# Two layers of linear attention and MLP on one core: queries projected in quarters, some rows kept on chip, new orders for every engine

## The chip, the cores and the metric

The kernel runs on one core of a Trainium2 chip. The metric is the device time in microseconds (us). Of the kernel before there are three timed runs, 989.24, 989.56 and 990.01 us, with a median of 989.56 us. Besides these there is one execution under the hardware profiler, which took 986.68 us; its trace spans 985.0 us from the first instruction to the last.

## What is computed

The input x has 2048 rows of 512 values. Two layers with the same weights are run, each an attention block and an MLP, both with a layer norm ahead and a residual:

```python
x = x + _A_ref(_layernorm(x), A_wqkv, A_w_phi, A_wo)
x = x + _B_ref(_layernorm(x), B_w1, B_w2)
x = x + _A_ref(_layernorm(x), A_wqkv, A_w_phi, A_wo)
x = x + _B_ref(_layernorm(x), B_w1, B_w2)
```

```python
phi_q = jnp.concatenate([_softmax(pq, axis=-1), _softmax(-pq, axis=-1)], axis=-1)
phi_k = jnp.concatenate([_softmax(pk, axis=-1), _softmax(-pk, axis=-1)], axis=-1)
kv = jnp.einsum("bhsf,bhsd->bhfd", phi_k, v)
z  = jnp.einsum("bhsf->bhf", phi_k)
num = jnp.einsum("bhqf,bhfd->bhqd", phi_q, kv)
den = jnp.einsum("bhqf,bhf->bhq", phi_q, z)[..., None] + 1e-6
o = num / den
```

There are 32 heads of 16. `pq` and `pk` are the queries and keys times a 16x16 matrix per head. kv and z are sums over all 2048 rows, so no row's output of the attention can be worked out before all keys and values have been. The MLP is `relu(x @ w1) @ w2` with 1792 hidden columns.

## The kernel before, in words

**Products.** Every matrix product is done in fp16 with each operand split into a high and a low half, and three matmuls per block (high x high, high x low, low x high; `PAIRS`). A weight W is split by `split`: ScalarE (ACT) writes the high half, scaled by a power of two, and VectorE (DVE) writes the rest (lines 417 and 419). The per-head matrix `w_phi` is folded into the key and the query weight at the start (`fold`, tiles `st_k`, `wt_k`, `pf_k`, `wk_h`, `wk_l` and the same with q). The scales come from the sums of squares of the weights (`square`, `squares_of`, line 370), added up over the partitions by a small matmul (`sb_k`, `sb_v`, line 380).

**Stages.** The 2048 rows are 16 chunks of 128; two chunks are a tile. Layer 0 begins with the *front*: for each chunk the layer norm, the transposed rows `xT` (`front_norm`), keys `pk`, values `pv`, and their part of kv (`gather`). Queries of the first chunks are projected in the front too (`query`, PSUM tile `pq`, line 624, twelve matmuls of 128x512). ACT copies `pq` to `qs` (line 785), SP's queue stores it to `q_dram` (788), and later `look` loads it as `ql` (869), the feature map on DVE, ACT and GpSimd (POOL) makes `e_q`, `fm_q` and `p_q` (653 to 688), and a DMA transpose makes `pT` (553). Rows whose query is projected late are stored to `xt_dram` (718) and loaded again as `xq` (777).

Then stands `opening(l)`, once per layer: the numerators `pn` of the first two chunks (890), the quotient `o`, its transpose `tr_o` (568) and `oT`, the product with wo (`pw`), the layer norm `xn_b`, its transpose `tr_b` and `yT`, and the remaining queries. In layer 0 the opening also holds `warming`: matmuls of the ones against themselves, whose result nobody reads (`warm_kv`, line 1558); `warm_y` are the same ahead of the first weights. After it come eight tiles of MLP steps: hidden products `ph` (1237, 1317), relu halves `h` (ACT 1000, DVE 1003), output products `py` (1351, 1394), and at their sides the attention of later tiles and, in layer 0, the keys and values of layer 1. Some steps use seven products instead of eight blocks; for these the sums of weight blocks `sums` are made on POOL (1110) and the sums of rows `ts`, `n_t`, `n_u` on POOL and ACT (961, 539, 542). `opening(1)` stands between the last tile of layer 0 and the first of layer 1. The last rows end with `mlp_out` (1369) and their store.

**What sets the order.** Every operation is a task of a `Plan` with its engine, its buffers and an estimated time. The tables in `ORDER` give each engine's sequence of tasks outright, as offsets into the list of tasks not yet taken; so each engine runs its own list strictly in that sequence, and an instruction that waits holds up all that stand behind it on its engine. SP issues all DMAs, the transposes among them, in one such list. Buffers rotate: the fp16 rows of the back half (`n16b`) have one place, so that ACT may write `n_t` only when the DMA transpose of the `n_b` before it has read that place.

Of the kernel before, what the change touches and what calls it, by code (L numbers as in the profile page):

```python
# [56 lines left out]
        "00000503111412100011109903770662a5203355172601416019402091430070220630063170300H0260D172320x600105016o00"  # L57
        "1310i1h00f001100000000001013100100004000124034010203406070020045010707992a1a020c370713504413320100001110"
        "00000020002000000000000000050700d00bh000j00k000000000000000000000001111122222222222122222222222022233330"
        "222222201000000001112201004400800b0000000000000011122223220111111111122220111111101112011110000000000003"  # L60
        "0500bbh0000000000000000600000000011122011122222222222333333333334445555555555144440333334445555555577777"
        "788888999aa09aaaaab0aaaa0999999aaaaaaaaaaa09999908006660550033333302222222222822222222222233320112222223"
        "33334444444444455555555555555104402229220pv11y1111111111111111100000000000000000000080035333331201g11000"
        "0aa00802004031010002002200570004000000020000201111122244444444444444444445556666666004550450444403333330"
        "22011111111100005006000000000000000000709000e00000000000000000b0E00000000z000000000000000000000000u00000"
        "000p00000000p00000000000000000000000000d00000000000000000000n0000000000000d0v000000000000000j00000000000"
        "00e0000000000000000000000000020v00w000000000000000000000000000o000000000000f0000000000000000000030000000"
        "000000030000000000000000h00000000000000050000k000k000000000000000000000000000011000000000030000000000000"
        "00000000000000000000000000000000000000000000000000000000000000000000000000000000000000000000000000000000"
        "00000000000000000000000000000000000000000000000000000000",  # L70
    DVE:
        "31203011i1103e4331212321g1001h4b03303304c0014070d01b000d0cWW00e0Sdg44e466e050Gbe5040390x20g1jf111f00g00i"
# [201 lines left out]
def tile_kernel(ctx: ExitStack, tc: tile.TileContext, x_in, wqkv, w_phi, wo, w1, w2, out):  # L274
# [165 lines left out]
    class Slots:  # L440
# [37 lines left out]
        def split(self, i):  # L478
            last = self.last
            split(lambda: self.raw(i, last), S_[f"s_{self.name}"], lambda: self.part(i, 0),  # L480
                  lambda: self.part(i, 1), self.n, [self.at_raw(i)], self.res[i], "")
# [1378 lines left out]
```

## Time and profile before

| | |
|---|---|
| median of the timed runs | 989.56 us (989.24 to 990.01) |
| profiled execution | 986.68 us, span 985.0 us |
| busy, share of the span | PE 98%, DVE 70%, POOL 61%, ACT 55% |
| instructions | PE 9514 matmuls, DVE 1396, ACT 1065, POOL 583 |
| moved by DMA | 182.21 MB, mean 185 GB/s |
| granted TensorE clock | 0.997 of full |

"Busy" is the time in which an engine had an instruction in work. A matmul of 128x512 is listed at 379 ns, but such matmuls start 216 ns apart, so PE busy means that it always had one under way. In the rows of the timeline the first number is the start and the second the duration, both in us; a bracket at the end gives how long the engine was idle just before and what ended that idle time. "x12" is the number of instructions in a row.

### The profile page before, as it was taken

What the parts mean: (1) busy time and instruction counts of PE and PEld (TensorE: products, weight loads), DVE (VectorE), ACT (ScalarE), POOL (GpSimd) and SP (SyncE); (2) the same over time, 40 slices, a digit from 0 to 9 for tenths busy, and PEclk for the clock granted to TensorE, in tenths of its full rate; (3) what the DMA queues carried; (4) which work ended last, traced back from release to release, by engine and by line L of the source; (5) the groups of instructions that cost most, each with busy time, mean ns of one, the idle gap of its engine ahead of it and who ended that gap; (6) DMA issues with size and microseconds to landing.
All of it is one profiled execution on the core that took longest, in us unless ns stands there. A gap on an engine that the chain in (4) does not pass through costs nothing.

```text
span 985.0 us, 23814 instructions
## 1 busy us (share of the span) xinstructions
PE 960.6 (98%) x9514; PEld 655.2 (67%) x9514; DVE 692.6 (70%) x1396; ACT 544.6 (55%) x1065; POOL 601.7 (61%) x583
## 2 busy tenths in 40 slices
PE   8999999999999999999999999979999999999997
PEld 5554555656565666666756565546666798898996
DVE  6889898986867768766564577846887665664554
ACT  7899975453454644544444344544455565564553
POOL 2586973667774856746345344455668788776553
PEclk9999999999999999999999999999999999999999
DMA  8357657659779797887758354899999977765541
GB/s 327 130 164 194 183 161 235 144 149 202 176 188 228 211 198 206 198 194 184 197 108 197 120 161 118 267 187 232 240 245 209 238 172 175 203 161 136 151 147 64
DMA packets 254575, 182.21 MB, mean 185 GB/s; under 512 B 184448, under 2 KB 191872, under 8 KB 254464
## 3 DMA queue, kind: packets, MB, share of 16 engines
q1 hardware_dynamic: 254464, 180.69, 71.2%
q8 instruction: 74, 1.21, 0.5%
q14 instruction: 37, 0.30, 0.1%
HBM read 103.84 MB, written 32.51 MB: 138 GB/s over the span
## 4 chain that ended last, share of the span: by engine, by line
PE 79%; DVE 7%; DMA 4%; ACT 3%; POOL 3%; issue 2%; SPq 1%; DVEq 0%; POOLq 0%; ACTq 0%
PE ph L1237 22%; PE py L1351 16%; PE py L1394 9%; PE pk L624 7%; PE pv L624 7%; PE pw L624 6%; PE pq L624 5%; PE ph L1317 2%; PE pn L890 2%; PE kv L762 2%; DMA oT<-n_o 1%; DVE fm_q L668 1%; DVE e_q L660 1%; SPq L553 1%; POOL p_q L688 1%
## 5 line engine op out<-in xcount | busy, mean ns | idle before, releaser
L1351 PE MATMUL py<-w,h 128*128 128x512 f16 x852 | 215.8, 379 | 0.0
L1237 PEld LDWEIGHTS <-s 128*128 128x128 f16 x2352 | 151.7, 98 | 34.9 <-issue 5.2
L1250 ACT ACTIVATE sn<-ph 128x128 f32<-128x128 f32 x294 | 80.3, 273 | 159.9 <-PE ph L1237 158.6
L624 PEld LDWEIGHTS <-xT 128*128 128x128 f16 x840 | 81.3, 98 | 92.9 <-issue 0.2
L1237 PEld LDWEIGHTS <-w 128*128 128x128 f16 x1764 | 110.7, 98 | 18.9 <-DMA yT<-n_b 2.2
L1351 PEld LDWEIGHTS <-h 128*128 128x128 f16 x852 | 75.5, 98 | 58.4
L1237 PE MATMUL ph<-yT,s 128*128 128x128 f16 x1176 | 97.6, 219 | 3.6 <-DVE ph L1256 2.2
L1237 PE MATMUL ph<-yT,w 128*128 128x128 f16 x1176 | 97.6, 219 | 3.0 <-ACT qs L785 3.0
L677 POOL TENSOR_TENSOR e_q<-e_q,fm_q 128x1024 f32<-128x1024 f32 x32 | 63.7, 1991 | 55.2 <-ACT fm_q L673 53.7
L1256 DVE TENSOR_TENSOR ph<-ph,sn 128x128 f32<-128x128 f32 x98 | 29.2, 298 | 85.5 <-PE ph L1237 42.0
L677 POOL TENSOR_TENSOR e_k<-e_k,fm_k 128x1024 f32<-128x1024 f32 x30 | 58.7, 1957 | 47.2 <-ACT fm_k L673 42.0
L688 POOL TENSOR_TENSOR p_q<-e_q,p_q 128x1024 f16<-128x1024 f32 x32 | 68.7, 2147 | 25.1 <-ACT p_q L684 24.1
L624 PE MATMUL pw<-wo_h,oT 128*128 128x512 f16 x256 | 81.2, 379 | 1.4 <-DMA oT<-n_o 1.4
L624 PE MATMUL pk<-wk_h,xT 128*128 128x512 f16 x256 | 81.3, 379 | 0.0
L624 PE MATMUL pv<-wv_h,xT 128*128 128x512 f16 x256 | 81.0, 379 | 0.0
L688 POOL TENSOR_TENSOR p_k<-e_k,p_k 128x1024 f16<-128x1024 f32 x30 | 65.3, 2177 | 21.4 <-ACT p_k L684 21.3
L1261 DVE TENSOR_TENSOR ph<-ph,sn 128x256 f32<-128x256 f32 x98 | 42.0, 429 | 49.5 <-PE ph L1237 49.2
L624 PE MATMUL pq<-wq_h,xq 128*128 128x512 f16 x208 | 66.8, 384 | 1.8 <-DMA xq<-xt_dram 1.8
L624 PEld LDWEIGHTS <-oT 128*128 128x128 f16 x384 | 36.7, 98 | 42.2 <-DMA oT<-n_o 1.7
L1003 DVE SCALAR_TENSOR_TENSOR h<-ph,h 128x512 f16<-128x512 f32 x71 | 48.0, 678 | 21.5 <-ACT h L1000 20.9
L1050 POOL TENSOR_TENSOR w<-r 128x256 f32<-128x256 f32 x41 | 31.4, 766 | 44.4 <-ACT r L1046 35.2
L1000 ACT ACTIVATE h<-ph 128x512 f16<-128x512 f32 x71 | 41.7, 591 | 26.5 <-DVE ph L1261 22.4
(241 smaller groups left out, 2294.7 us busy)
## 6 DMA issues: line engine op xcount, KB each, us to landing
s<-s_dram SPq DMA_DIRECT2D x98, 512.0 KB, 4.4
q_dram<-qs SPq DMA_DIRECT2D x32, 256.0 KB, 3.4
ql<-q_dram SPq DMA_DIRECT2D x32, 256.0 KB, 3.7
xt_dram<-xT SPq DMA_DIRECT2D x26, 256.0 KB, 4.4
xq<-xt_dram SPq DMA_DIRECT2D x26, 256.0 KB, 3.8
xe<-in_A_x_dram SPq DMA_DIRECT2D x16, 256.0 KB, 5.3
x<-in_A_x_dram SPq DMA_DIRECT2D x16, 256.0 KB, 3.5
x_dram<-x SPq DMA_DIRECT2D x16, 256.0 KB, 4.4
```

What stands on the lines that cost most here:

```text
L624: nc.tensor.matmul(pm.ap, xT.ap[:, a, k, :], W.ap[b][:, k, :], start=(k == 0 and i == 0), stop=(k == KC - 1 and i == 2))
L677: (nc.vector if fast else nc.gpsimd).tensor_tensor(e3, e3, sm.unsqueeze(2).to_broadcast([P, 2 * n, DH]), op=ALU.mult)
L688: (nc.vector if fast else nc.gpsimd).tensor_sub(p16.ap[:, 1, cols], ef, p16.ap[:, 0, cols])
L1000: nc.scalar.activation(h[0].ap, at(), AF.Relu)
L1003: add(DVE, 0.607, lambda: nc.vector.scalar_tensor_tensor(h[1].ap, at(), 0.0, h[0].ap, op0=ALU.max, op1=ALU.subtract), reads=[ph, h[0]], wr ...
L1050: nc.gpsimd.tensor_sub(rf.ap[:, :2, :], r.ap.rearrange("p (a b) -> p a b", a=4)[:, ::3, :], block(1).unsqueeze(1).to_broadcast([P, 2, P]))
L1237: nc.tensor.matmul(at(r), weight_of(i, b, kk, s, summed), rows_of(y, i, a, kk), start=(first and kk == 0 and n == 0), stop=(kk == 1 and n ...
L1250: nc.scalar.activation(saved(i), at(2), AF.Copy)
L1256: add(DVE, 0.27, lambda: nc.vector.tensor_tensor(at(3), at(1), saved(2), op=ALU.add), reads=[(ph, 1), (sn, 2)], writes=[(ph, 3)], boost=10 ...
L1261: add(DVE, 0.40, lambda: nc.vector.tensor_tensor(wide(ph), wide(ph), wide(sn), op=ALU.add), reads=[(sn, 0), (sn, 1)], writes=[(ph, 0), (ph ...
L1351: nc.tensor.matmul(py.ap, h[a].ap.rearrange("p j t -> p (j t)")[:, cols], W2.at(b, fs[j], slice(0, D)), start=(begins and j == k == 0), st ...
L1394: nc.tensor.matmul(py.ap[:, 256 * r:256 * r + 256], left[a], right[b], start=(s == 0 and r == 0 and k == 0), stop=(last and k == 2), skip_ ...
```

## The change

1. **Queries in four pieces.** `project` takes `cuts`; a query's twelve matmuls are four tasks of three, so that the order may put other work between them. The queries of the first six chunks of layer 0 stay whole.
2. **First queries of layer one stay in SBUF.** For chunks 0 to 3 of layer 1 (`straight`) ACT copies `pq` into the `ql` tile itself: four stores to `q_dram` and four loads from it are gone.
3. **Rows not copied through memory.** `direct` now holds for chunks 12 to 15 of layer 0 and 14 and 15 of layer 1 too: six stores to `xt_dram` and six loads from it are gone. Each of these transfers is 256 KB.
4. **Key weight asked for first**: both halves of `st_k` are issued ahead of `phi` and the second chunk's rows. The first chunk's rows still go first in SP's list.
5. **Squares** of a weight are taken in one or two ACT instructions in place of four.
6. **W2's first four pairs** are split on ACT and POOL: two more ACT instructions each, and `tensor_sub` on POOL (new line 425) in place of DVE's line 419.
7. **Warming**: all 29 matmuls in `opening(0)` go, and 6 of 26 at the start.
8. **The last product by halves** (`last_rows`): the last six matmuls of 128x512 become twelve of 128x256 into two PSUM banks, with one DVE instruction and one store for each half.
9. All five `ORDER` tables are new. `opening(1)` now lists the queries of chunks 2, 3, 14 and 15 ahead of the layer norm.

```diff
     def direct(l, c):
-        return l == 0 and c < NCH - LATE
+        return soon(c) or c >= NCH - 2 * CPT if l == 0 else c >= NCH - CPT
+    def straight(l, c):
+        return l == 1 and c < 2 * CPT
...
-    def project(xT, W, tag, name):
+    def project(xT, W, tag, name, cuts=1):
...
-            for k in range(KC):
+            for k in range(part * KC // cuts, (part + 1) * KC // cuts):
...
-        add(PE, 2.59, go, reads=[xT, W], makes=[pm])
+        for part in range(cuts):
+            add(PE, 2.59 / cuts, partial(go, part), reads=[xT, W], makes=[] if part else [pm],
+                writes=[pm] if part else [])
...
-        pq = project(xT, Wq, tag, f"pq_{n}")
-        qs = tiles(fr, "qs", [P, D], F32, f"qs_{n}")
+        pq = project(xT, Wq, tag, f"pq_{n}", cuts=1 if l == 0 and soon(c) else 4)
+        kind = "ql" if straight(l, c) else "qs"
+        qs = tiles(fr, kind, [P, D], F32, f"{kind}_{n}")
...
+        if pool:
+            add(ACT, 0.16 + cols / 1160, lambda: nc.scalar.activation(w(), w(), AF.Copy, scale=s.ap),
+                reads=[s], writes=reads)
+            add(ACT, 0.16 + cols / 1160, lambda: nc.scalar.activation(hi(), w(), AF.Copy),
+                reads=reads, writes=[(res, f"h{key}")])
+            add(POOL, 0.14 + cols / 523, lambda: nc.gpsimd.tensor_sub(lo(), w(), hi()),
+                reads=[*reads, (res, f"h{key}")], writes=[(res, f"l{key}")])
+            return
...
-            square(lambda k=k: f32_piece(b)[:, k, :], lambda k=k: W.ap[1][:, k, :], sq, k, 512,
+            square(lambda ks=ks: f32_piece(b)[:, ks, :], lambda ks=ks: W.ap[1][:, ks, :], sq, i, 512 * n,
...
-        if idle:
-            warming("kv0", 10, before())
+        if l == 1:
+            for c in [*range(CPT, 2 * CPT), *range(NCH - CPT, NCH)]:
+                query(l, c, "h")
```

The order shows what that moves. On **PE in the opening of layer 0** the last numerators of chunk 1 (`pn_1`) are followed by the turns `tr_o` of the two chunks and the product with wo (`pw_0`). Before, from the turn of chunk 1 on:

```order
L568 MATMUL tr_o_1_2170<-ident,o_1_2150 128x128 x4
L1558 LDWEIGHTS ones
L1558 MATMUL warm_kv_6_2122<-ones 128x256
...
L624 LDWEIGHTS oT_0_2163
L624 MATMUL pw_0_2185<-wo_h,oT_0_2163 128x512
```

and after, from the last numerators on:

```order
L916 MATMUL pn_1_0_2093<-rhs_0_2004,pT_1_1891 128x68
L634 LDWEIGHTS xT_12_1396
L634 MATMUL pq_12_2029<-wq_h,xT_12_1396 128x512
...
L577 MATMUL tr_o_0_2118<-ident,o_0_2067 128x128 x4
L634 LDWEIGHTS xT_12_1396
L634 MATMUL pq_12_2029<-wq_h,xT_12_1396 128x512
...
L577 MATMUL tr_o_1_2135<-ident,o_1_2114 128x128 x4
L634 LDWEIGHTS oT_0_2130
L634 MATMUL pw_0_2142<-wo_h,oT_0_2130 128x512
```

Pieces of three matmuls of the query of chunk 12, read from its own `xT`, now stand where groups of warming stood; another piece of that query stands between the numerators, and one of chunk 11 behind `pw`. Before, the queries of chunks 11 and 12 ran whole ahead of the numerators.

On **ACT in the opening of layer 1**, at the layer norm of chunks 0 and 1 (`xn_b`, `n_b`) and the sum of their rows (`n_t`). Before:

```order
L539 ACTIVATE n_b_0_8961<-xn_b_0_8943 128x512
L785 ACTIVATE qs_9_8984<-pq_9_8947 128x512
L602 ACTIVATE xn_b_1_8989<-x_1_8010,stat_b_1_8963 128x512
L539 ACTIVATE n_t_0_9039<-ts_0_8998 128x512
L785 ACTIVATE qs_10_9041<-pq_10_8971 128x512
L539 ACTIVATE n_b_1_9043<-xn_b_1_8989 128x512
L664 ACTIVATE e_q_4_8930<-e_q_4_8930,inv_q 128x1024
L785 ACTIVATE qs_11_9070<-pq_11_9014 128x512
```

and after:

```order
L548 ACTIVATE n_b_0_8876<-xn_b_0_8871 128x512
L806 ACTIVATE qs_6_8884<-pq_6_8797 128x512
L611 ACTIVATE xn_b_1_8895<-x_1_7760,stat_b_1_8867 128x512
L548 ACTIVATE n_b_1_8945<-xn_b_1_8895 128x512
L806 ACTIVATE qs_7_8953<-pq_7_8862 128x512
L548 ACTIVATE n_t_0_8965<-ts_0_8925 128x512
L676 ACTIVATE e_q_4_8892<-e_q_4_8892,inv_q 128x1024
L806 ACTIVATE qs_8_8975<-pq_8_8936 128x512
```

The norm of chunk 1 and one more copy of a query have moved ahead of `n_t`, and the queries around it are 6 to 8 where they were 9 to 11.

On **POOL around the opening of layer 0**, from the feature map of chunk 1's query (`p_q_1`) on. Before:

```order
L688 TENSOR_TENSOR p_q_1_1553<-e_q_1_1026,p_q_1_1553 128x1024
L677 TENSOR_TENSOR e_q_2_1899<-e_q_2_1899,fm_q_2_1898 128x1024
L688 TENSOR_TENSOR p_q_2_2198<-e_q_2_1899,p_q_2_2198 128x1024
L605 TENSOR_TENSOR stat_b_0_2219<-stat_b_0_2219,nhalf 128x1
L677 TENSOR_TENSOR e_q_3_2012<-e_q_3_2012,fm_q_3_2011 128x1024
L605 TENSOR_TENSOR stat_b_1_2242<-stat_b_1_2242,nhalf 128x1
L688 TENSOR_TENSOR p_q_3_2267<-e_q_3_2012,p_q_3_2267 128x1024
```

and after:

```order
L700 TENSOR_TENSOR p_q_1_1763<-e_q_1_1073,p_q_1_1763 128x1024
L425 TENSOR_TENSOR w_0_140<-w_1_141,w_0_140 128x1024
L689 TENSOR_TENSOR e_q_2_1862<-e_q_2_1862,fm_q_2_1861 128x1024
L700 TENSOR_TENSOR p_q_2_2132<-e_q_2_1862,p_q_2_2132 128x1024
L689 TENSOR_TENSOR e_q_3_2011<-e_q_3_2011,fm_q_3_2010 128x1024
L614 TENSOR_TENSOR stat_b_0_2179<-stat_b_0_2179,nhalf 128x1
L1136 TENSOR_TENSOR sums_2035<-sums_2035 128x256
L1136 TENSOR_TENSOR sums_1983<-sums_1983 128x256
L614 TENSOR_TENSOR stat_b_1_2198<-stat_b_1_2198,nhalf 128x1
L700 TENSOR_TENSOR p_q_3_2184<-e_q_3_2011,p_q_3_2184 128x1024
L425 TENSOR_TENSOR w_1_141<-w_2_142,w_1_141 128x1024
```

Two of the four W2 subtractions stand here (`w_0`, `w_1`), the other two some seven instructions apart behind them, and the norm's `stat_b_0` now follows `e_q_3`.

More of the change, by code (lines that the diff above doesn't have):

```diff
@@ L62 @@
[L62 to L66, printed above, removed]
```

196 lines of the change are left out of this document (104 added, 92 removed).

## Prediction

> **What bounds the kernel now.** First the page's busy times, then a table of windows cut at the stages, to see where the busiest engine is not busy.
>
> ```profile
> PE 960.6 (98%) x9514; PEld 655.2 (67%) x9514; DVE 692.6 (70%) x1396; ACT 544.6 (55%) x1065; POOL 601.7 (61%) x583
> core 0: us, PE busy (x) PEld busy (x) DVE busy (x) ACT busy (x) POOL busy (x), PEclk, DMA share, GB/s
> 0.00:22.00 22.00, 17.11 (x109) 12.62 (x110) 13.00 (x41) 15.60 (x36) 5.18 (x17) 1.00 0.88 316
> 22.00:157.00 135.00, 135.00 (x984) 71.40 (x985) 122.54 (x222) 117.05 (x178) 93.24 (x64) 1.00 0.59 172
> 157.00:174.00 17.00, 15.79 (x175) 11.30 (x174) 13.38 (x34) 8.35 (x13) 9.88 (x7) 1.00 0.83 261
> 174.00:205.00 31.00, 30.23 (x248) 19.36 (x246) 29.05 (x48) 16.32 (x23) 20.88 (x18) 1.00 0.65 145
> 205.00:640.00 435.00, 431.42 (x4034) 272.45 (x4034) 302.33 (x596) 205.72 (x396) 241.60 (x209) 1.00 0.73 184
> 640.00:672.00 32.00, 26.06 (x231) 15.27 (x230) 16.64 (x38) 14.43 (x29) 17.88 (x17) 0.95 0.96 201
> 672.00:970.00 298.00, 295.55 (x3662) 245.68 (x3661) 187.75 (x409) 164.28 (x386) 208.50 (x248) 1.00 0.76 187
> 970.00:985.00 15.00, 9.43 (x85) 7.08 (x83) 7.93 (x14) 2.88 (x6) 4.53 (x6) 0.92 0.14 54
> ```
>
> PE is the bound. Its idle time is the window less its busy time: 4.89 us at the start, none in layer 0's front, 1.21 and 0.77 in and behind the first opening, 3.58 in the long middle, 5.94 in the second opening, 2.45 behind that and 5.57 in the last 15 us. That is 24.4 us in all, so no reordering can win much over 20 us, and a change wins only where PE idles, crawls, or does work that nobody reads. The matmuls that compute the result stay the same but for the very last six, which become twelve of half the width. So I go through the four places.
>
> **Start.** The rows are PE's, then two of ACT's on the squares of the value weight, and one group of squares of W2.
>
> ```profile
> 8.26 1.09 PE L1505 MATMUL wt_k<-ident,st_k 128*128 128x128 f32 x8 [0.23 <-DMA st_k<-in_A_wqkv_dram]
> 15.06 0.36 PE L380 MATMUL sb_v<-sq_v,ones 128*128 128x4 f32 x2 [1.09 <-DVE stat_a L607]
> 21.89 1.15 PE L1505 MATMUL wt_q<-ident,st_q 128*128 128x128 f32 x8 [1.38 <-ACT wT_q L1510]
> 14.02 0.63 ACT L370 ACTIVATE wv_l<-st_v 128x512 bf16<-128x512 f32 x1
> 14.54 0.20 ACT L370 ACTIVATION_READ_ACCUMULATOR wv_l<-st_v 128x1 f32 x1
> L370 ACT ACTIVATE w<-w x9: 1041/1049/1692, 39.4 to 98.6; 128x1024 bf16<-128x1024 f32 x6, 128x1792 bf16<-128x1792 f32 x3
> ```
>
> PE is held twice behind ACT's list: `sb_v` needs the last square, finished at 14.74, and `wt_q` waits 1.38 us. A square of 512 columns takes 0.62 us from start to start with its read; two of 1024 save a little (1.05 + 0.19 against 1.24), and one of 2048, by the step from 1024 to 1792 columns (0.64 us for 768) about 1.90 + 0.20, saves about 0.4 of 2.5. More is won because `sb_v` now stands behind all of `pf_k` on PE, so that the splits of the key weight no longer wait for a value square between them. The second half of the key weight, now one place earlier in SP's list, can win no more than PE waits for it, with what follows. The bounds are 0 (ACT's table load now waits for the first rows, and eats the gain) and the 0.23 + 1.09 + 1.38 us that the three brackets hold, 2.7. I take the two larger brackets at about two thirds of their 2.5 us: **-1.7**.
>
> **First opening.** The group row is that of the warming; a piece of the chain of waits gives a query's twelve matmuls; POOL's row shows how loaded it was.
>
> ```profile
> L1558 PE MATMUL warm_kv<-ones x29: 272/273/273, 158.3 to 170.1; 128*128 128x256 f16 x29
> 620.25 2.59 PE pq L624 x12
> 157.20 1.29 PE L890 MATMUL pn<-rhs,pT 128*128 128x68 f16 x36
> 170.88 1.39 PE L1317 MATMUL ph<-yT,w 128*128 128x128 f16 x22 [0.42 <-DVE yT L577]
> 159.74 1.93 POOL L677 TENSOR_TENSOR e_q<-e_q,fm_q 128x1024 f32<-128x1024 f32 x1 [12.08 <-ACT fm_q L673]
> ```
>
> From the numerators at 157.20 to the first hidden product at 170.88 PE follows a chain through DVE, ACT and back, 13.7 us long; warming only filled it. Four pieces of three query matmuls, 12 x 2.59/12 = 2.6 us, move from ahead of that chain into it. If the chain keeps its length, everything after comes 2.6 us earlier. It could also shrink: the warming's stream is 29 x 0.108 = 3.1 us (half a 512-column matmul each). It could stretch: `stat_b_0` now stands behind `e_q_3` on POOL, up to 1.9 us by POOL's row, of which a part falls into idle time. Bounds -3.1 and -0.7 (2.6 less 1.9); I take **-2.6**, since DVE ahead of it has three splits fewer and so does not hold the numerators.
>
> **W2's pairs** stand in and behind this opening.
>
> ```profile
> L419 DVE SCALAR_TENSOR_TENSOR w<-w,s_w,w x9: 1272/1539/2123, 80.8 to 187.5; 128x1024 f16<-128x1024 f32 x6, 128x1792 f16<-128x1792 f32 x3
> L688 POOL TENSOR_TENSOR p_q<-e_q,p_q 128x1024 f16<-128x1024 f32 x32 | 68.7, 2147 | 25.1 <-ACT p_q L684 24.1
> 195.01 2.30 POOL L688 TENSOR_TENSOR p_q<-e_q,p_q 128x1024 f16<-128x1024 f32 x1 [0.66 <-ACT p_q L684]
> 195.25 2.62 DVE L659 TENSOR_TENSOR e_q<-ql,fm_q 128x512 f32<-128x512 f32 x1
> 185.37 0.68 DVE L659 TENSOR_TENSOR e_q<-ql,fm_q 128x512 f32<-128x512 f32 x1
> 205.76 2.78 PE L1317 MATMUL ph<-yT,w 128*128 128x256 f16 x24 [1.53 <-DVE h L1003]
> ```
>
> DVE loses 4 x 1.27 = 5.1 us, three of the four ahead of the numerators and one behind. POOL gains 4 x 2.15 = 8.6 us, at the price of `p_q`, the same shape; ACT gains 8 instructions of 1.05 (the 1024-column row above), 8.4 us. Between 157 and 205 POOL is busy for 30.8 of 48 us and ACT for 24.7; with three of the four pairs POOL has 37.2 and ACT 31.0, so there is room, and the first pair falls into POOL's 12.08 us of idle time. But the two `e_q` rows show what POOL's work does to DVE: beside a POOL instruction of that size 0.68 us became 2.62. Three such meetings would cost DVE 3 x 1.94 = 5.8 us, net of the one saved split +4.5, and PE waits for DVE at 205.76. If none meet, the 1.53 there may go. Bounds: -1.5 and +4.5; most POOL instructions of these 48 us meet no two-input DVE work, so I take **+0.5**, nearer the lower end. If the cover on POOL is gone, PE waits for W2's low halves themselves; that is a rival below.
>
> The Trainium skill has a rule that speaks against this edit: by "SBUF — State Buffer", section "Who interferes with whom", VectorE with two inputs in SBUF and GpSimd exclude each other, and the later one is blocked until the first ends. The two rows agree with it: DVE's instruction ends at 197.87, 0.56 behind POOL's end at 197.31, about the time that it takes by itself. If that rule struck at every pair, the sum would take the upper bound above.
>
> **Second opening.** PE's two stalls and the query after them, ACT's and SP's rows in that place, and the transposes of `yT` between 635 and 660.
>
> ```profile
> 649.77 0.49 PE L1237 MATMUL ph<-yT,w 128*128 128x128 f16 x6 [2.98 <-ACT qs L785]
> 652.13 0.61 PE L624 MATMUL pq<-wq_h,xq 128*128 128x512 f16 x1 [1.49 <-DMA xq<-xt_dram]
> 652.13 4.11 PE pq L624 x12
> 648.60 0.63 ACT L539 ACTIVATE n_t<-ts 128x512 f16<-128x512 f32 x1 [6.48 <-DMA yT<-n_b]
> 642.46 5.82 SPq L553 DMA_TRANSPOSE pT<-p_q  x1
> DMA to landing us min/median/max: 4.1/6.0/8.0
> ```
>
> The bracket at 649.77 names a copy of a query, but ACT's list shows the cause: ACT stood 6.48 us at `n_t`, until the transpose of `n_b` had landed, and the copy that frees PE's bank was queued behind. That transpose took up to 8.0 us while the DMA engines were 0.96 busy; SP sat 5.82 us on the next one, so `xq` was issued late, and PE waited 1.49 us more. Then twelve matmuls took 4.11 us where 2.59 is usual.
>
> After the change, the order puts the norm of chunk 1 and one more copy ahead of `n_t`, and on PE 39 query matmuls and two groups of numerators between `pw` and the first `ph`, where 36 and one stood: 3 x 0.216 + 0.38 = 1.0 us more cover. The `xq` that was late is no longer behind that transpose, and the clock's loss goes with the idle time: 1.0 + 1.49 + (4.11 - 2.59) = 4.0 us. Twelve of the removed 256 KB transfers belong to layer 1's queries; if the transpose lands in the 4.1 us of the faster one, the remaining 2 us go as well. Bounds 0 (the wait only moves to the next transpose) and -7.5 (the stage's 5.94 us and the slow matmuls' 1.5). I take **-4.5**, near the worked 4.0.
>
> **Tail.** DVE's and POOL's last rows.
>
> ```profile
> 978.00 0.47 DVE L1426 SCALAR_TENSOR_TENSOR v<-py,inv,w 128x256 f32<-128x256 f32 x1
> 978.56 2.50 POOL L1434 TENSOR_TENSOR x<-x,v 128x512 f32<-128x512 f32 x2 [6.37 <-DVE v L1426]
> 980.59 1.53 DVE L1369 SCALAR_TENSOR_TENSOR x<-py,inv,x 128x512 f32<-128x512 f32 x3
> ```
>
> The last sums wait for POOL's two additions, which end at 981.06, not for PE; so halving the last product wins nothing. DVE now does one more 0.5 us instruction ahead of what POOL needs: bounds 0 and +1.3 (one whole POOL addition), taken **+0.5**.
>
> **Sum.** -1.7 - 2.6 + 0.5 - 4.5 + 0.5 = -7.8 us. From the profiled execution's 986.68 (span 985.0 and 1.68 around it) this gives 978.9; the median of the timed runs is 2.88 above that execution, so 989.56 - 7.8 = **981.8 us**.
>
> **Rivals.** (A) *The chains set both openings.* If DVE and the transposes, not the place of PE's work, decide when `ph` begins, the queries' pieces fill holes that were waits anyway. For it: ACT's 6.48 us ended with a DMA. Against: PE's order has 1 us more cover, and twelve transfers are gone. It keeps the -0.7 of the first opening, -1.5 of the second and half the start: -3, giving 986.5.
>
> (B) *POOL becomes the bound behind the first opening: slower.* The price is its 8.6 us of subtractions straight on the path, and DVE's net 4.5 from being held, in place of the 0.5 taken: 13.1 - 8.3 = +4.8, giving 994.4 at the worst, and 991.1 if three quarters of it show (9.8 - 8.3 = +1.5), the size that I give the rival; it is slower than before from 8.3 us on. It decides from the point where W2's low half of a step comes after PE is through that step's product with the high half; the stall at 205.76 says that there is no slack in that stage already. Against it stands POOL's 17 us of room in 48.
>
> (C) *All waits go*: start -2.7, first opening -3.1, W2 -1.5, second -7.5, tail 0: -14.8, giving 974.8.
>
> (D) *The clock falls in the first opening.* In the second, 2.98 and 1.49 us of idle time with 0.9 of work between made twelve matmuls 1.52 us slower. Without warming, PE has holes in the first opening: 0.33 us twice and 0.42 before, and up to about 1.5 us where 18 warming matmuls filled the wait around `tr_b`. If these suffice, one such loss comes back: 983.3. The Trainium skill, "TensorE: Matmul & The Clock Gate", section "Part 1: The HAM clock gate (the "warmup" mystery)", states that the clock is halved after an idle window of about 3.4 us; the slow query above agrees with it, and by that rule the holes here are too short.
>
> (E) *It doesn't do what it says*: the first rows still go ahead of the key weight, so the start keeps its time. Then 983.5, inside the forecast's own range.
>
> **Chances.** Forecast with D and E, 979 to 985: 0.58. A, 985 to 989: 0.17. C, below 979: 0.13. B and other slips above 989: 0.12. The range leaves out about 0.2: **975.5 to 989.0**. A measurement of this kernel can tell about 0.2% (2 us) from no change, that is outside 987.6 to 991.5. Faster by that: 0.58 + 0.13 + 0.11 of A = 0.82; within: 0.06 of A and 0.03 of B = 0.09; slower: 0.09.
>
> **What would show it.** Start: `pk` begins at about 15.5 instead of 17.3. First opening: numerators about 4.3 us earlier, and the same 13.7 us from there to the first `ph`. W2: no bracket in front of PE's `py` that names POOL. Second opening: no `pq` at half rate, PE idle under 2 us there, ACT's wait at `n_t` below 4. Tail: POOL's last addition ends later after PE's end than 1.2 us. The forecast is wrong if ACT still waits 6 us at `n_t`, or if DVE's two-input instructions in the first tile grow past 2 us each.

## The result and the profile after

The changed kernel takes **979.83 us** (median of 4 runs, 979.15 to 981.66), against 989.78 us (989.24 to 991.13, 4 runs) for the kernel before beside it. The ratio is 0.990, 95% interval 0.9882 to 0.9918: 1% faster, by 10 us, where -7.8 us and 981.8 us were forecast. Timed again later, beside the last experiment, it gained 6.8 us (981.21 against 987.96 us, ratio 0.9935, interval 0.9916 to 0.9954), so the gain is known to 7 to 10 us. Its profiled execution took 979.16 us with a span of 977.4, 7.6 us less than before.

The table of windows of the kernel after, cut where its own stages begin and end:

```profile
core 0: us, PE busy (x) PEld busy (x) DVE busy (x) ACT busy (x) POOL busy (x), PEclk, DMA share, GB/s
0.00:22.00 22.00, 16.37 (x98) 12.48 (x98) 12.85 (x40) 14.01 (x23) 4.65 (x17) 0.92 0.79 272
22.00:155.50 133.50, 133.04 (x975) 70.65 (x976) 117.28 (x217) 118.00 (x176) 96.08 (x66) 1.00 0.62 176
155.50:173.50 18.00, 15.30 (x157) 9.61 (x156) 16.18 (x34) 10.50 (x15) 11.77 (x9) 1.00 0.65 186
173.50:204.00 30.50, 28.76 (x245) 18.69 (x243) 24.12 (x44) 22.88 (x29) 24.08 (x18) 1.00 0.63 134
204.00:633.00 429.00, 427.81 (x4021) 271.07 (x4019) 298.35 (x590) 203.63 (x392) 238.81 (x208) 1.00 0.68 178
633.00:665.00 32.00, 28.20 (x263) 17.02 (x262) 19.58 (x44) 16.46 (x33) 18.47 (x17) 1.00 0.89 200
665.00:963.00 298.00, 297.12 (x3662) 245.99 (x3660) 190.71 (x412) 164.90 (x388) 212.86 (x250) 1.00 0.78 189
963.00:977.40 14.40, 8.55 (x80) 6.84 (x78) 8.04 (x14) 2.58 (x5) 5.91 (x7) 0.89 0.19 73
```

PE's idle time is now 5.6 us at the start (4.9 before), 2.7 and 1.7 around the first opening (there before's busy time held 3 us of warming), 1.2 in the middle (3.6 before), 3.8 in the second opening (5.9), 0.9 behind it (2.5). The start got worse, and the middle, which the forecast left alone, got better.

To put the terms beside this, both traces are compared at points of **equal useful work**: each matmul row counts its columns (0.216 us for 512 at full clock, 0.111 for an fp32 transpose of 128), warming counts nothing, and the point is when so much had been started. The table gives how the lead of before changes over each stretch, minus being a gain; the last column holds the other profiles of the experiments below whose code in that stretch is the changed kernel's, with their number. Another way of counting the small matmuls shifts an entry by up to 0.1 us.

| stretch, by useful work | forecast | the two profiles | other profiles, same code there |
|---|---|---|---|
| start, 0 to 40 us | -1.7 | +0.94 | +0.80 to +3.81 (8) |
| front, 40 to 140 | 0 | +0.14 | +0.13 to +0.14 |
| first opening, 140 to 156 | -2.6 | -1.68 | -1.68 to -1.69 (4, without e1) |
| W2 and first tile, 156 to 201 | +0.5 | +0.23 | +0.22 to +0.24 (4, without e1) |
| middle, 201 to 590 | 0 | -2.25 | -0.36 to -2.23 (9) |
| second opening, 590 to 643 | -4.5 | -3.94 | -4.11 to -5.59 (9) |
| behind it, 643 to 920 | 0 | -1.33 | -0.33 to -1.65 (10) |
| tail, 920 to the end | +0.5 | +0.29 | +0.25 to +0.39 (10) |
| sum | -7.8 | -7.6 | |

So the total came out near the forecast partly by luck, with errors that offset each other: start, front, openings and W2 came out 4.0 us worse together than forecast, and 3.6 us were gained in stretches that were priced at nothing. In e1 the first opening and the first tile are apart in the table because PE ran at half rate there, from about 171 to 174 us; over both stretches e1 comes out as the first profile does, for it did not meet the wait of 1.74 us shown below. The rows behind the table, stage by stage.

**Start**, in the kernel after: PE's first wait, ACT's first instructions, SP's issue of `phi`.

```profile
8.09 0.50 PE L381 MATMUL sb_phi<-sq_phi,ones 128*128 128x1 f32 x2 [2.19 <-ACT squares L371]
18.03 0.38 PE L634 MATMUL pk<-wk_h,xT 128*128 128x512 f16 x1
```

```profile
3.81 1.28 ACT L611 ACT_TABLE_LOAD   x1 [3.81 <-DMA xe<-in_A_x_dram]
5.77 0.81 ACT L611 ACTIVATE xn_a<-xe,stat_a 128x512 f32<-128x512 f32 x1 [0.68 <-DVE stat_a L616]
7.68 0.26 ACT L371 ACTIVATE squares<-phi 128x64 bf16<-128x64 f32 x1 [1.10 <-DMA phi<-in_A_w_phi_dram]
7.94 1.04 ACT L371 ACTIVATE wk_l<-st_k 128x1024 bf16<-128x1024 f32 x1
```

ACT's table load, which needs no data, stands in the list behind the wait for the first rows, at 3.81; `phi`, now behind 1 MB of key weight, lands about 7.6; the key weight's first square begins at 7.94, where before it began at 5.21. `pk` begins at 18.03, not at the 15.5 forecast. But ACT's list is not all of it:

```profile
10.18 1.75 PE L1551 MATMUL wt_k<-ident,st_k 128*128 128x128 f32 x8
11.28 1.27 ACT L1556 COPY wT_k<-wt_k 128x512 f32<-128x512 f32 x2 [1.17 <-PE wt_k L1551]
```

The same eight transposes took 1.09 us before (the row at 8.26 in the prediction). Behind its wait of 2.19 us PE ran at half rate (PEclk is 0.50 from 9 to 11 us), and ACT, done with its squares, waited 1.17 us for them. All nine profiles with this start show it (1.69 to 1.92 us), the two with before's start (before and e8) do not (1.09). Where `tr_a` behind it still ran near full rate (0.60 to 0.69 us: the first profile, e6, e10) the start is +0.8 to +1.1; where that was slow too (1.02 to 1.06 us: e3, e4, e5, e7, e9, e12) it is +1.5 to +3.8. Before's own start lies 0.97 us apart in its two profiles.

**First opening**, DVE's and POOL's rows at the numerators, then PE's:

```profile
155.10 2.42 DVE L671 TENSOR_TENSOR e_q<-ql,fm_q 128x512 f32<-128x512 f32 x1
172.32 2.62 DVE L672 TENSOR_TENSOR e_q<-fm_q,ql 128x512 f32<-128x512 f32 x1
```

```profile
154.86 2.11 POOL L689 TENSOR_TENSOR e_q<-e_q,fm_q 128x1024 f32<-128x1024 f32 x1 [1.03 <-ACT fm_q L685]
171.80 2.58 POOL L425 TENSOR_TENSOR w<-w,w 128x1024 f16<-128x1024 f32 x1
```

```profile
155.73 0.92 PE L916 MATMUL pn<-rhs,pT 128*128 128x68 f16 x24
159.10 0.41 PE L577 MATMUL tr_o<-ident,o 128*128 128x128 f32 x2 [0.40 <-DVE dn L924]
170.06 1.63 PE L1343 MATMUL ph<-yT,w 128*128 128x128 f16 x24 [1.17 <-ACT qs L806]
175.59 0.54 PE L916 MATMUL pn<-rhs,pT 128*128 128x68 f16 x12 [1.74 <-DVE yT L586]
```

The numerators came earlier by 1.47 us although the start was later, but the quotients waited: DVE's next subtraction, 0.68 us by itself, lasted 2.42 until POOL's product beside it had ended. From the numerators to the end of the first 24 `ph` it is 15.8 us (155.73 to 171.52) where before it was 14.9 (157.20 to 172.11). Behind it the same happens again: POOL's new W2 subtraction of 171.80 holds DVE's `e_q` of 172.32 for 2.62 us, and PE waits 1.74 us at 175.59. The 1.53 us at 205.76 of before are gone, so this stretch comes out even.

**Second opening**: PE's two waits, ACT's `n_t`, SP's transpose ahead of it.

```profile
644.64 0.49 PE L1263 MATMUL ph<-yT,w 128*128 128x128 f16 x6 [1.83 <-ACT qs L806]
648.81 0.51 PE L1263 MATMUL ph<-wk_h,s 128*128 128x128 f16 x6 [1.09 <-DMA wk_h<-n_t]
```

```profile
642.43 0.63 ACT L548 ACTIVATE n_t<-ts 128x512 f16<-128x512 f32 x1 [2.16 <-DMA yT<-n_b]
```

```profile
637.54 1.23 SPq L562 DMA_TRANSPOSE yT<-n_b  x1
```

ACT waits 2.16 us at `n_t` (6.48 before), the transpose lands 4.9 us after its issue (8.0 before), PE waits 1.83 and 1.09 (2.98 and 1.49 before), and no `pq` runs at half rate: PEclk is 1.00 in this window.

**Tail**: DVE's last additions still wait for POOL.

```profile
973.61 0.88 DVE L1414 SCALAR_TENSOR_TENSOR x<-py_last,inv,x 128x256 f32<-128x256 f32 x2 [1.10 <-POOL x L1478]
```

### The profile page after: what moved, and what is told of

The parts are those of the page before. It is cut to its first block, busy times and chain, and to the rows that moved or that the text cites. A ratio compares the mean times of both kernels' runs of the same rounds, so it can differ in the third digit from the quotient of the medians.

```text
span 977.4 us, 23693 instructions
## 1 busy us (share of the span) xinstructions
PE 955.1 (98%) x9485; PEld 652.3 (67%) x9485; DVE 687.1 (70%) x1390; ACT 553.0 (57%) x1057; POOL 612.6 (63%) x587
## 5 line engine op out<-in xcount | busy, mean ns | idle before, releaser
L634 PEld LDWEIGHTS <-xT 128*128 128x128 f16 x912 | 87.5, 98 | 97.9 <-issue 0.4
L634 PE MATMUL pq<-wq_h,xq 128*128 128x512 f16 x160 | 54.1, 379 | 0.0
```

The costliest lines, as they stand in the source:

```text
L634: nc.tensor.matmul(pm.ap, xT.ap[:, a, k, :], W.ap[b][:, k, :], start=(k == 0 and i == 0), stop=(k == KC - 1 and i == 2))
```

## The experiments

All but the last two were run once. The totals of such runs differ by up to 3 us through the start alone (most of that goes with the clock), so each is read in the stretch that it touches. In the diffs `MOVES` takes the task with the first number out of an engine's sequence and puts it ahead of the task with the second.

**e1_phi_between.** `phi` goes between the halves of the key weight.

```diff
-        writes=[phi], kb=32).deps.setdefault(key_load, False)
+        writes=[phi], kb=32)
+MOVES = {SP: [(3, 1)]}
```

> The changed kernel with one place of SP's list as before: phi is issued between the two halves of the key weight, not behind both. In the changed kernel phi lands at about 7.7 us, PE stands 2.19 us at sb_phi, and the first value product begins at 22.78 against 22.87 before, with the useful matmul work 1.2 us behind. Theory 1 (phi's late landing is the start's loss): phi lands near 5.3, the bracket at sb_phi falls below 1 us, and the front runs 1.0 to 1.5 us earlier. Rival (the table load and the norm ahead of the squares on ACT are the loss): phi lands earlier, but ACT comes to its square only after the norm, at about 6.6, so that sb_phi still waits over 1 us and less than 0.7 us is won.

980.85 us, and the start is +0.98, as late as ever. PE's wait for `sb_phi` fell to 0.53 us, but ACT then waits at the other half of the weight:

```profile
3.75 1.28 ACT L617 ACT_TABLE_LOAD   x1 [3.75 <-DMA xe<-in_A_x_dram]
9.45 1.06 ACT L377 ACTIVATE wk_l<-st_k 128x1024 bf16<-128x1024 f32 x1 [2.67 <-DMA st_k<-in_A_wqkv_dram]
```

The late landing of `phi` alone is not the cause; the rival, that ACT comes late to its squares, fits better, though not in its own sign (PE's wait was to stay over 1 us).

**e2_phi_and_act.** As e1, and on ACT one square of the key weight and the square of `phi` go ahead of the first norm.

```diff
+MOVES = {SP: [(3, 1)], ACT: [(23, 19), (11, 19)]}
```

> As the run with phi between the halves, and ACT's list begins as before: first half of the key weight squared, phi squared, then the first norm, so that the table load no longer waits for the first rows. Theory 1 (phi's landing is all): no more than 0.3 us beyond the run with phi alone. Rival (ACT's order is the loss): at least 0.7 us more than that run, and together 1.2 us or more, that is the front as early as before or earlier.

978.48 us. ACT's rows:

```profile
0.80 1.28 ACT L377 ACT_TABLE_LOAD   x1 [0.80 <-PEq L1880]
5.02 1.06 ACT L377 ACTIVATE wk_l<-st_k 128x1024 bf16<-128x1024 f32 x1 [2.94 <-DMA st_k<-in_A_wqkv_dram]
```

The start is -0.45 against before, 1.4 us better than the changed kernel's first profile, though PE's clock fell here too (the eight `wt_k` take 1.97 us). So the two orders together are worth at least this; with SP's alone nothing was won, and a move on ACT without SP's was not run.

**e3_features_later.** The feature map of chunk 3 goes behind the first opening's chain (moves on DVE, ACT and POOL).

```diff
+MOVES = {DVE: [(648, 568), (650, 572)], ACT: [(649, 576), (651, 583), (653, 583)],
+         POOL: [(652, 785), (581, 785)]}
```

> The changed kernel with the feature map of chunk 3's query put behind the chain of the first opening: on DVE its two-input subtractions behind the first oT, its sum behind the first norm, and ACT's and POOL's parts with it. In the changed kernel DVE's e_q there took 2.42 us beside a POOL instruction in place of 0.68 and the quotients began at 158.04, 1.6 us after their numerators. Theory 2 (the chain was held by DVE being locked out by POOL): the quotients follow the numerators within 0.4 us and the first ph begins 1.0 to 1.7 us earlier than 170.06. Rival (the chain behind the quotients is bound elsewhere, by ACT or the transposes): the quotients come earlier but the first ph moves less than 0.5 us. Chunk 3's numerators come later, which may cost some of it in the first tile under either.

986.43 us; the opening and the stretch behind it take 4.2 us more than before, where the changed kernel gains 1.5. The quotients do follow the numerators now, but the subtractions meet POOL elsewhere, each later on the chain:

```profile
162.13 2.62 DVE L678 TENSOR_TENSOR e_q<-fm_q,ql 128x512 f32<-128x512 f32 x1
174.71 2.66 DVE L677 TENSOR_TENSOR e_q<-ql,fm_q 128x512 f32<-128x512 f32 x1
177.30 2.61 DVE L678 TENSOR_TENSOR e_q<-fm_q,ql 128x512 f32<-128x512 f32 x1
```

From the numerators to the first `ph` it is 14.0 us against 14.3, so nothing like the expected 1.0 us was won. PE also ran at half rate twice (about 174 to 178 and 181 to 185 us), which is part of the 4.2 us. So the run shows the lock and not the price of that one meeting.

**e4_split_later.** POOL's second W2 subtraction goes behind three sums.

```diff
+MOVES = {POOL: [(668, 678)]}
```

> The changed kernel with one POOL instruction moved: the subtraction of W2's second pair goes behind three short sums. In the changed kernel it ran from 171.80 to 174.38, DVE's e_q beside it took 2.62 us, and PE waited 1.67 us at the numerators at 175.59. Theory 2 (the lockout by POOL makes this stall): e_q falls to about 0.7 to 1.4 us and the stall shrinks by 1.0 to 1.9 us. Rival (PE waits for something else, yT as its bracket says, and e_q only looks late): the stall stays within 0.3 us of 1.67 though e_q is short.

981.46 us, with a start 2.0 later, where the clock fell (the last section). PE's wait at the numerators, 1.74 us in the changed kernel, is

```profile
176.16 0.53 PE L922 MATMUL pn<-rhs,pT 128*128 128x68 f16 x12 [0.34 <-DVE yT L592]
```

and the stretch gains 1.40 us more. One meeting of POOL and DVE thus costs 1.4 us in this stretch, and goes with the order alone.

**e5_w2_on_dve.** The four W2 pairs go back to DVE; ACT's and POOL's parts are empty tasks. DVE does them at 153.81, 171.39, 187.70 and 201.09 us, near POOL's places in the changed kernel (151.69 to 193.21); in the kernel before they ran earlier, at 130.0, 136.0, 141.8 and 175.7 us.

```diff
-            add(POOL, 0.14 + cols / 523, lambda: nc.gpsimd.tensor_sub(lo(), w(), hi()), ...
+            add(POOL, 0, lambda: None, ...)
+            add(DVE, 0.12 + cols / 940, lambda: nc.vector.scalar_tensor_tensor(
+                lo(), w(), s.ap, hi(), op0=ALU.mult, op1=ALU.subtract), ..., ahead=AHEAD.pop(0))
```

> The changed kernel with the four W2 pairs' low halves back on DVE, in one instruction each, and without the two extra ACT instructions; all else in its order. Theory 2 (what the POOL edit costs is the lockout at one place, 1.9 us lost at 173.65, and what it wins is PE's wait for DVE at the end of the first steps, 1.5 us at 205.76 before): the stall ahead of the second tile's numerators falls to about 0.6 us, a stall of 1 to 1.5 us behind 195 returns, and the stretch from 150 to 210 loses 5 to 6 us in all, as with the edit (5.8). Rival (the edit is a plain cost of about 2 us): the stretch loses under 4.5 us.

983.34 us; opening and first tile cost 3.6 us more than in the changed kernel. DVE's split is itself held beside POOL, and PE has three waits:

```profile
158.09 0.88 PE L923 MATMUL pn<-rhs,pT 128*128 128x68 f16 x23 [1.57 <-DVE rhs L852]
177.65 0.54 PE L923 MATMUL pn<-rhs,pT 128*128 128x68 f16 x12 [2.69 <-DVE yT L593]
211.28 0.55 PE L923 MATMUL pn<-rhs,pT 128*128 128x68 f16 x12 [2.00 <-DVE o L934]
```

Neither expectation came: the stall at the second tile's numerators, which was to fall to about 0.6 us, is 2.69. With the splits at these late places W2 on POOL is a gain of 3.6 us; what DVE would cost at before's early places no run shows.

**e6_traffic_back.** For chunks 0 to 3 of layer 1 the 256 KB stores and loads come back as copies that nobody reads (the loads go to a spare place in memory).

```diff
+            add(SP, 0.47, lambda: nc.sync.dma_start(q_dram[c], qs.ap), reads=[qs], writes=[q_res[c]], kb=256, ahead=...)
+            add(SP, 0.47, lambda: nc.sync.dma_start(spare.ap, q_dram[c]), reads=[q_res[c]], writes=[spare], kb=256, ahead=...)
```

> The changed kernel with 8 of the removed transfers of 256 KB put back as traffic only, at about the places where the kernel before had them: for chunks 0 to 3 of layer 1 the query is stored to memory as well, and copied from there to another place in memory; nobody reads it. Theory 3 (the second opening won about 4 us because fewer transfers stand ahead of the transposes): ACT's wait at n_t grows by over 1.5 us and PE loses 1.5 to 3 us more between 620 and 665. Rival (it won by order: a piece of query work more ahead of ph, the norm of chunk 1 ahead of n_t): PE loses less than 0.7 us more. Control: the same stretch in the four kernels run so far, which left it alone, differs by up to 1.2 us from the profile of the changed kernel.

983.86 us; the second opening gains only 0.31 us over before, where it gains 3.94 to 5.59 without the copies. But the rows show another way than contention. SP's and PE's:

```profile
628.54 4.37 SPq L908 DMA_DIRECT2D spare<-q_dram  x2
637.14 3.92 SPq L567 DMA_TRANSPOSE pT<-p_q  x1
642.22 1.24 SPq L567 DMA_TRANSPOSE yT<-n_b  x1
```

```profile
642.93 1.34 PE L928 MATMUL pn<-rhs,pT 128*128 128x68 f16 x24 [4.12 <-DMA pT<-p_q]
```

The second copy waits in SP's list for the first one (both write `spare`; the waits of SP give 3.3 us), so the transpose `pT` is issued at 637.14 where it was 631.44, and PE waits 4.12 us for it and then runs at half rate to about 646.6. The transpose of `n_b` landed by ACT's `n_t` at 646.89, 4.7 us after its issue, as fast as without the copies (4.9). So the run shows what a held place in SP's list costs; that traffic slows a transpose it does not show.

**e7_queries_whole.** The first of four pieces does all twelve matmuls.

```diff
-            for k in range(part * KC // cuts, (part + 1) * KC // cuts):
+            for k in range(0 if part else KC):
```

> The changed kernel with every query's twelve matmuls at the place of its first piece, all else as ordered. Theory 4 (the pieces win by filling the holes of the chains): in the first opening nine matmuls of chunk 12's query come ahead of the numerators and the first ph follows about 1.9 us later; in the second opening the holes come back too: 2 to 5 us slower in all. Rival (the holes are short anyway, and the order rather than the pieces counts): less than 1 us in each opening.

989.29 us, no better than before. Front, first opening and first tile together lose 1.9 us against the changed kernel, and the second opening gains 0.50 us where it gains 3.94 to 5.59. A whole query early needs its bank early:

```profile
621.09 0.38 PE L634 MATMUL pq<-wq_h,xT 128*128 128x512 f16 x1 [1.57 <-ACT ql L806]
628.68 0.19 PE L916 MATMUL pn<-rhs,pT 128*128 128x68 f16 x1 [0.69 <-ACT rhs L841]
```

Of what it loses in the second opening, 4.1 us lie between 619 and 638 us, mostly in such waits (1.57, 0.69, 0.29 and 0.64 us). The new orders of both openings rest on the pieces; in the first one part of the loss is half rate (about 174 to 177 us), and how much was not separated.

**e8_before_no_warming.** The kernel before without its 29 matmuls in the opening.

```diff
-            for _ in range(n):
+            for _ in range(n if tag == "y1" else 0):
```

> The kernel before with its 29 warming matmuls of the first opening left out, and nothing else changed. Theory 5 (they only filled waits): from the numerators at 157.20 to the first ph the same 13.7 us within 0.3, and the time of the kernel before within its spread. Rival (they keep the clock up): the product with wo or the first ph runs at half rate in part, 1.0 to 2.0 us longer. A third outcome, a shorter chain by up to 1.0 us, would say that warming stood in the way.

984.37 us. In the opening:

```profile
170.67 0.27 PE L1317 MATMUL ph<-yT,w 128*128 128x128 f16 x2 [0.68 <-ACT yT L573]
171.40 1.39 PE L1317 MATMUL ph<-yT,w 128*128 128x128 f16 x22 [0.45 <-DVE yT L577]
```

Opening and first tile gain 0.73 us over before, and nothing runs at half rate there. From the numerators (158.17) to the row at 171.40 it is 13.2 us against 13.7: the third outcome, warming stood a little in the way. The other 1.6 us of its span are stretches where it has before's own code: start +0.97, middle -0.77, second opening -0.75, behind it -1.03.

**e9_factor_earlier.** The small copy `fm_q` of chunk 2 goes ahead of two others on ACT, so that POOL's product at 154.86 may begin earlier.

```diff
+MOVES = {ACT: [(640, 548)]}
```

> The changed kernel with one move on ACT, about the first opening: the small copy fm_q of chunk 2 (0.25 us) goes ahead of the two rhs copies, into the 0.81 us that ACT waits for them. Theory (DVE's held subtraction ate the first opening's gain): POOL's product e_q of chunk 2 begins about 153.8 where it began at 154.86, ends 1.0 earlier, DVE's subtraction e_q of chunk 3 is held 1.4 us where it was 2.42, and the quotients, tr_o, pw and the first ph come 1.0 us earlier against the numerators: from the first pn to the first quotient 1.3 us where it was 2.3, and 1.0 us off the time from there on. Rival (the chain behind is set by ACT and PE's order, so an earlier quotient meets the next wait): the quotients move, the first ph does not, 0 to -0.3 us. Second rival: ACT's small copy delays rhs, the numerators come 0.25 us later, +0.25. A single look varies by up to 2 us at the start, so the verdict is read from the rows between 150 and 175 and not from the total.

978.81 us, with a start 1.8 later. POOL's product did move, and now holds DVE one instruction earlier:

```profile
156.19 1.98 DVE L851 TENSOR_TENSOR rhs<-rhsf,rhs 128x272 f16<-128x272 f32 x2
158.09 0.68 DVE L677 TENSOR_TENSOR e_q<-ql,fm_q 128x512 f32<-128x512 f32 x1
```

The opening gains 0.55 us more (-2.23), half of what was expected, since `rhs` is late for the numerators instead.

**e10_last_whole.** The last product in one piece.

```diff
-                        nc.tensor.matmul(py.ap[:, cols], ..., W2.at(b, fs[j], cols), ...)
+                        nc.tensor.matmul(py.ap, ..., W2.at(b, fs[j], slice(0, D)), ...)
```

> The changed kernel with the last product in one piece again: six matmuls of 128x512 into one bank in place of twelve of 128x256 into two; the two additions and stores by halves stay. Theory (the last additions wait for POOL, not for PE): the time from the start of the last product to the end of the span stays at 6.9 us, within 0.2, and DVE's bracket ahead of the last two additions still names POOL. Rival (the halves let the first addition begin early): 0.4 to 0.7 us more, and the bracket names PE.

978.05 us. From the start of the last product to the end of the span it is 6.83 us, against 6.86 in halves (970.54 to 977.4):

```profile
969.47 1.46 PE L1411 MATMUL py_last<-w,h 128*128 128x512 f16 x6
972.54 0.88 DVE L1417 SCALAR_TENSOR_TENSOR x<-py_last,inv,x 128x256 f32<-128x256 f32 x2 [1.10 <-POOL x L1481]
```

The halves win nothing; POOL's addition sets the end.

**e11_three_moves** and **e12_after_again.** The moves of e2, e4 and e9 together, and beside it the changed kernel as it is, each timed six times with the same runs of before (median 987.96 us of 11).

```diff
+MOVES = {SP: [(3, 1)], ACT: [(23, 19), (11, 19), (640, 548)], POOL: [(668, 678)]}
```

> The changed kernel with the three mends that the runs so far point to, and no others: the start as in e2 (phi between the key weight's halves, ACT's first square of the key weight and the square of phi ahead of the first norm), ACT's fm_q of chunk 2 ahead of the rhs copies as in e9, and POOL's second subtraction of W2 three sums later as in e4. Theory (the three losses are separate and add up): -1.4 at the start, -0.5 at the first opening and -1.4 at the numerators behind it, -3.3 together, so about 976.5 against 979.8 for the median of the changed kernel: ratio to the changed kernel about 0.9967, to the kernel before 0.9866. Rival (what is won at the start is waited for again at the first opening or at the next product of rows from memory, as e2's single look did not show but could): -0.5 to -1.5, about 978.5 to 979.3. In both cases it beats both kernels or equals the changed one; it is slower only if the second opening's transposes fall worse.

> The changed kernel as it is, as the measure for the run beside it and for how far one look varies. Theory: 979 to 981 in the median; in its profile the start lies 0 to 2 us behind that of the first profile, there is a stall of about 1.5 us near 361 us or none, and the second opening lies 0 to 1.7 us ahead, since these three places differed among the kernels that share their code there. Rival (the single looks differ because of their edits): this profile agrees with the first one within 0.3 us everywhere.

e11 takes **977.41 us** (974.65 to 980.35), ratio to before 0.9897, interval 0.9875 to 0.992; e12 takes 981.21 us (980.42 to 982.49), 0.9935, interval 0.9916 to 0.9954. All six of e11 lie below all six of e12; the medians are 3.8 us apart. e11 beats both kernels. The 3.8 us bear out the theory's 3.3 and not the rival's 0.5 to 1.5.

By stretches of e11's one profile, the start is -0.19 (1.1 better than the first profile of the changed kernel) and opening and first tile -2.28 (0.83 better), where e4 and e9 alone gave 1.40 and 0.55. The missing 1.1 us go to the clock:

```profile
168.37 2.51 PE L1349 MATMUL ph<-yT,w 128*128 128x128 f16 x24 [1.17 <-ACT qs L812]
```

These matmuls took 1.63 us in the changed kernel, behind the same wait. PEclk is 0.50 from 169 to 172 us, and from here to the numerators at 173.25 that costs 1.6 us, a part of which would have been waiting (0.34 us were left in e4).

e12's median lies just above the expected 979 to 981. Its profile differs from the first one of the same code in three places: 2.9 us at the start (up to 2 were expected), 1.3 us near 350, and 1.2 us the other way in the second opening. The wait near 350 is in seven of the twelve profiles with the new orders (1.08 to 1.44 us) and missing in five. PE's rows of the two that cost:

```profile
23.48 0.66 PE L1551 MATMUL wt_q<-ident,st_q 128*128 128x128 f32 x4 [2.02 <-ACT wT_q L1556]
352.48 0.93 PE L916 MATMUL pn<-rhs,pT 128*128 128x68 f16 x24 [1.16 <-DMA pT<-p_q]
```

So a stretch in one profile is known to 1 to 3 us at the start, and to 1 to 2 us wherever PE comes close behind a DMA transpose.

## Why the prediction was right in sum and wrong in parts

- **Start, -1.7 forecast, +0.8 to +3.8 found: wrong.** The step that failed is "the second half of the key weight, now one place earlier in SP's list, can win no more than PE waits for it", with a lower bound of 0: a loss was not in the bounds. The table load's wait was named, but only as what "eats the gain". Two things stood in its place. e2 and e11 show that the order of ACT's list together with SP's place of `phi` is worth 1.1 to 1.4 us. And PE ran its transposes at half rate in all nine profiles, with ACT waiting 1.17 us for them in the first. The sum had no term for the clock here, and rival D looked at the first opening alone. Six warming matmuls were dropped here as well; what share each has, and why the clock was low, stays open, for no run kept this start at full rate (in e3, e4, e5 and e7 the four `wt_k` ahead of the wait for `sb_phi` were slow already, 1.09 us against 0.63). The brackets that were to go moved on: `wt_q` now waits 1.50 us for ACT.
- **First opening, -2.6 forecast, -1.7 found: mis-sized.** The query pieces entered the chain as said and "the chain keeps its length" failed by 0.9 us (15.8 against 14.9), the whole of what is missing, for DVE is held beside POOL. The sign given was numerators 4.3 us earlier; they came 1.47 earlier, as the start was late instead of early. What "would make the forecast wrong", DVE's two-input instructions past 2 us, came about twice, at 155.10 and 172.32, and e4 and e9 price the meetings at 1.4 and at least 0.55. The Trainium skill's rule in "SBUF — State Buffer", section "Who interferes with whom", that one blocks the other, agrees with each of these rows (0.68 us became 2.42 to 2.66).
- **W2, +0.5 forecast, +0.2 found: right,** by both of its parts: one new meeting (+1.9 in lost PE time) and the stall at 205.76 gone (-1.7). Rival B did not come: no `py` waits for POOL. That DVE would cost 3.6 us more at the late places of this order (e5) was not seen; whether the edit wins over before's early places stays open.
- **Second opening, -4.5 forecast, -3.9 found (-4.1 to -5.6 in the other profiles): right.** ACT's wait shrank to 2.16 us and the half rate went, as told. PE's idle time did not fall under the 2 us given as a sign: it is 3.8, for in place of the 1.49 us at `xq` PE now waits 1.09 for `wk_h`. That the removed transfers made the transpose land faster stays **open**: e6 put traffic back and the transpose landed as fast as without it. In before another transpose was issued 1.9 us behind that of `n_b` and five transfers (four of 256 KB, one of 512) within 3.2 us ahead of it, in the changed kernel two of 256 KB and no such transpose; no run separates these. e7 shows that without pieces the gain is 0.5.
- **Warming.** In the first profile and in e8 (0.73 us gained) dropping it cost no clock, as told. But rival D did come in the first opening of other profiles: in e1 and e11 PE fell to half rate behind the waits of 0.46 us at `tr_b` and 1.17 at `ph`, which the first profile has too (0.47 and 1.17). In e11 it cost about 1.6 us, the 1.5 that the rival was priced at; in e1 it cost nothing, for it took the place of the wait of 1.74 us behind it.
- **Middle and behind the second opening, 0 forecast, -3.6 found: missed.** Part of it is one profile against another: e8 gains 1.8 us there over before with before's own code, and the changed kernel's repeats gain -0.4 to -2.2 in the middle against the -2.25 of its first profile. What remains, 1 to 2 us, fits two waits of PE that before and e8 both have, at 271.63 (0.86 us, for DVE's `h`) and at 784.60 (1.38, for DVE's `ph`), and no profile with the new orders; which move removed them was not tested.
- **Tail, +0.5 forecast, +0.3 found: right.** POOL's last addition ends 1.56 us behind PE where it was 1.17, and e10 shows that the halves do nothing.

## What to carry to other kernels

An order that wins by filling waits is to be read on each engine from the first instruction on: a table load or a square that needs little is better not put behind one that waits for rows. The granted clock belongs in that reading: a wait of PE can cost a second time behind it. Two-input work of DVE and anything large on POOL should be put where the one that matters goes first; moving a meeting by one instruction only changes who is late, so look at what stands on either side. And a profile is one throw: compare stretches at equal work over several profiles before pricing anything below 2 us.

## What the runs showed of the hardware

Matmuls fell to half rate after waits much shorter than the forecast took for the limit. In e12, the windows behind the 2.02 us wait that ended at 23.48 (columns as in the table of windows above, PEclk the third from the end):

```profile
23.00:25.00 2.00, 1.52 (x9) 1.03 (x10) 2.00 (x4) 2.00 (x2) 0.00 (x0) 0.95 0.97 398
25.00:27.00 2.00, 2.00 (x7) 0.63 (x5) 1.86 (x7) 1.28 (x4) 0.55 (x1) 0.50 1.08 436
27.00:29.00 2.00, 2.00 (x11) 1.26 (x10) 0.15 (x1) 0.56 (x2) 0.55 (x1) 0.69 0.61 230
```

The clock is at 0.50 from 25 to 27 us; eight steps of `pv` take 0.43 us instead of 0.216, 1.7 us in all, more than half of that start's 2.9. The same place fell to half rate in e4 (waits of 1.92 us) and e7 (2.02), and not in the first profile (1.50), e6 (1.44), e10 (1.48), e9 (1.72), e3 (1.74), e5 (1.75), e2 and e11 (1.85) or e1 (1.88). The Trainium skill, "TensorE: Matmul & The Clock Gate", section "Part 1: The HAM clock gate (the "warmup" mystery)", speaks of an idle window of about 3.4 us; here a wait of 1.92 us with short transposes behind it was enough, and the measurement decides. In the first opening of e1 and e11 waits of 0.46 and 1.17 us were followed by half rate, in the first profile nearly the same waits (0.47 and 1.17) were not; what decides this no run here shows. Nor does before's slow query fit a limit of 3.4 us without work, as the prediction has it: the clock fell between 651 and 652 us, and PE had worked about 0.9 us between its waits of 2.98 and 1.49.
